# Attention into two expert layers on one core: the experts' token lists by 9 blocks of 32 places, and the first expert's second-layer weights fetched behind the first gather

## The chip, the core and the metric

The kernel runs on 1 core of a Trainium2 chip. The metric is the device time of one execution in microseconds. Five engines take part, each with its own queue of instructions: TensorE (PE in the rows; PEld is its weight load), the vector engine (DVE), ScalarE (ACT), GpSimd (POOL) and SyncE (SP), which only issues transfers here. An instruction waits for what it needs from other engines, and all that stands behind it on its engine waits with it. TensorE's granted clock is 1 at 2.4 GHz and 0.5 at 1.2 GHz.

## The reference

```
scores = q @ k.T / 8                          # 4 x 8 heads, 576 x 576, head size 64
attn = softmax over the 32 largest of each row
x = attn @ v, as 2304 tokens x 512
# first experts: 8 of them, 288 tokens each
logits = x @ w_gate                           # 2304 x 8
for idx in argsort(-logits.flatten()):        # greedy, best pairs first
    tok, e = idx // 8, idx % 8
    if tok has an expert or e has 288 tokens: continue
    assigned[tok] = e
out[tokens of e] = relu(x[tokens of e] @ w1[e]) @ w2[e]     # 512 -> 1024 -> 512
# second layer
h = out @ w_in;  result = (h * cos(h)) @ w_out              # 512 -> 2048 -> 512
```

## The kernel before

The program has four stages. Attention ends at about 453 us with x in HBM and the logits on chip. The first experts follow until about 760 us, then the second layer.

**The greedy assignment** (class `Search`) isn't done pair by pair. A round finds, by four comparisons with 24 thresholds each, how far the tokens' best logits may be taken until one expert has its 288 tokens; that expert is closed, and its number is written to `k.order` (lines 836 to 838). Each comparison is a chain: the vector engine compares (line 769), TensorE counts in 18 products (line 797), the vector engine decides (lines 801, 802), TensorE spreads the answer (line 804), and the vector engine moves the thresholds (line 808). Lines 814 to 828 then select the tokens and find the closed expert.

**The list of an expert** (`place`) follows its round. Each of the 128 partitions holds 18 tokens. The vector engine masks the expert's tokens and counts along the partition (lines 857 to 860), TensorE adds the counts of the partitions ahead (line 864), and `pos` is then the place of each token among the 288. It is split into a block and a place in it: 3 blocks of 96. Lines 873 and 874 make a mask of the block times the token's number (in two parts), line 877 a mask of the place, in two halves of 9 tokens, 18 products (line 883) put each token's number at its place, and `i96` gets it as 96 partitions x 3 columns for each expert.

**Rounds, lists and products share the engines.** `search` and `place` are generators: each `yield` is a point at which they hand over, and `tick()` runs each waiting generator up to its next one. `tick(1)` runs the first alone. Ahead of the first products only the search runs; within the products `m1` calls `tick()` four times in each of its first 8 iterations (`MID`) and twice in the later ones. So the order of instructions on each engine is fixed when the program is built.

**The products** (`m1`) run over 8 experts x 8 groups of 128 hidden features, 64 iterations. In one, `h` makes 12 products of the first layer (line 1184) and `y` 12 of the second (line 1199), two iterations later. `gather(e)` brings the expert's rows of x in three indirect transfers by GpSimd (line 1161), once the list is there; `xt` turns them with TensorE (line 1174) in one of the later iterations. ScalarE evicts what `h` made (line 1190) and the vector engine makes its low part (line 1191).

**Weights** come as float32 and are used as a high and a low part. `fetch` issues a transfer of 512 KB on SyncE's queue (line 1070) into one of three buffers (the last of expert 0's first layer goes to a buffer of its own, `r64`); `split` converts it: ScalarE makes the high part `wu` (line 1084), the vector engine or GpSimd the low part (line 1087, or 1266 where it is put off to the next iteration). Which expert's weights are fetched stands in `k.order`, which SyncE loads first (line 1058). In the order of use the first expert has four first-layer pieces, then four of the second layer, then the next expert's.

Of the kernel before, what the change touches and what calls it, by code (L numbers as in the profile page):

```python
# [34 lines left out]
E, CAP, NTOK = 8, 288, B * S  # L35
# [6 lines left out]
def constants(k, tmp):  # L42
    nc, cp = k.nc, k.cst
    G, V = nc.gpsimd, nc.vector

    def iota(name, shape, pattern, base, cm, dt=F32, pool=cp):
        t = pool.tile(shape, dt, name=name)
        G.iota(t, pattern=pattern, base=base, channel_multiplier=cm, allow_small_or_imprecise_dtypes=True)
        return t
# [15 lines left out]
    k.io3 = iota("io3", [128, 3], [[1, 3]], -100, 0)  # L65
    k.io16 = iota("io16", [128, E], [[1, E]], 16, 0)
    k.io128 = iota("io128", [128, 128], [[1, 128]], 0, 0, BF)

# [666 lines left out]
class Search:  # L735
# [36 lines left out]
    def search(s):  # L772
        k, nc, sb, rb = s.k, s.nc, s.sb, s.rb
        PEe, V, A = nc.tensor, nc.vector, nc.scalar
# [3 lines left out]
        tile = lambda nm, shape, dt=F32, nb=2: sb.tile(shape, dt, name="r" + nm, bufs=nb)  # L778
        pc, pq, pn = rb[:NS, 0:E], rb[:, E:E + 1], rb[:, 16:16 + 18 * E]
        for r in range(E):  # L780
# [8 lines left out]
            else:  # L789
# [5 lines left out]
                for z in range(NR):  # L795
# [10 lines left out]
                    if z < NR - 1:  # L806
                        w = tile("v", [128, 18])
# [21 lines left out]
            new = full  # L829
# [2 lines left out]
                V.tensor_tensor(new, full, s.full, op=OP.subtract)  # L832
            s.full = full

            t = tile("t", [128, E])
            V.scalar_tensor_tensor(t, new, 1.0, k.io16, op0=OP.mult, op1=OP.mult, accum_out=k.codes[:, r:r + 1])
            V.tensor_scalar(t[:1, 0:1], k.codes[:1, r:r + 1], -16.0, 0.0, op0=OP.add, op1=OP.max)
            V.tensor_scalar(k.order[:, r:r + 1], t[:1, 0:1], float(E - 1), None, op0=OP.min)
            s.gens.insert(0 if r == 0 else len(s.gens), s.place(r, GO if r == 0 else k.A, new))
            if r == 0:  # L840
                nc.gpsimd.tensor_copy(k.A, GO)
            s.closed += 1
# [4 lines left out]
    def place(s, r, A, new):  # L847

        k, nc, sb, rb = s.k, s.nc, s.sb, s.rb
        PEe, V = nc.tensor, nc.vector  # L850
        t18 = lambda nm, dt=F32: sb.tile([128, 18], dt, name="p" + nm)
        if r:
            yield
        while s.placed < r:
            yield
        AA = sb.tile([128, 18, E], BF, name="pAA")
        V.tensor_tensor(AA, A, new[:, None, :].to_broadcast([128, 18, E]), op=OP.mult)
        Ae, cs, pos, j, lo, jm, t1 = t18("A"), t18("cs", BF), t18("pos"), t18("j"), t18("lo", BF), t18("jm"), t18("t")
        V.tensor_reduce(Ae, AA, X, OP.add)
        V.tensor_tensor_scan(cs, k.onesf[:, :18], Ae, 0.0, OP.mult, OP.add)  # L860
        for _ in range(2 if r else 1):
            yield
        pr, pt = rb[:, 176:177], rb[:96, 180:186]
        PEe.matmul(pr, k.tri, cs[:, 17:18], start=True, stop=True)
        yield 1
        V.tensor_scalar(pos, cs, pr, -1.0, op0=OP.add, op1=OP.add)
        V.tensor_scalar(t1, pos, 96.0, None, op0=OP.is_ge)
        V.scalar_tensor_tensor(j, pos, 192.0, t1, op0=OP.is_ge, op1=OP.add)
        V.scalar_tensor_tensor(lo, j, -96.0, pos, op0=OP.mult, op1=OP.add)
        V.scalar_tensor_tensor(jm, Ae, -100.0, j, op0=OP.mult, op1=OP.add)  # L870
        yield
        ob, R = sb.tile([128, 18, 3], BF, name="pob"), sb.tile([128, 18, 2, 3], BF, name="pR")
        V.tensor_tensor(ob, jm[:, :, None].to_broadcast([128, 18, 3]), k.io3[:, None, :].to_broadcast([128, 18, 3]), op=OP.is_equal)
        V.tensor_tensor(R, ob[:, :, None, :].to_broadcast([128, 18, 2, 3]), k.tab[:, :, :, None].to_broadcast([128, 18, 2, 3]), op=OP.mult)
# [10 lines left out]
        h = sb.tile([96, 3], F32, name="ph")  # L885
        V.tensor_copy(h, pt[:, 3:])
        V.scalar_tensor_tensor(h, pt[:, :3], 64.0, h, op0=OP.mult, op1=OP.add)
        V.tensor_scalar(k.i96[:, 3 * r:3 * r + 3], h, float(NTOK - 1), None, op0=OP.min)
        s.placed += 1

        if r == 0:
            V.tensor_tensor(s.slot, pos, Ae, op=OP.mult)
        else:
            V.scalar_tensor_tensor(t1, pos, float(CAP * r), Ae, op0=OP.add, op1=OP.mult)
            V.tensor_tensor(s.slot, s.slot, t1, op=OP.add)
        if r == E - 1:
            s.gens.append(s.finish())

    def finish(s):

        k, nc, sb, rb = s.k, s.nc, s.sb, s.rb
        PEe, V = nc.tensor, nc.vector
# [14 lines left out]
        pt = rb[:, 192:228]  # L917
# [97 lines left out]
class FFN:  # L1015
# [148 lines left out]
    def m1(s, sb, ps, yT):  # L1164
# [50 lines left out]
        def fetch():  # L1215
            while s.fetched < min(last, s.done + 2 * s.RAW) and s.ready():
                e = s.units[s.fetched // 2][1]
                if rt and e < E and rt.closed <= e:
                    return
                s.fetch(1)  # L1220
# [9 lines left out]
                fetch()  # L1230

        while rt and rt.closed < 1:
            tick()
        s.half_pi, s.sin, s.least = (s.yp.tile([128, 1], F32, name=nm) for nm in ("hpi", "sin1", "least"))
        nc.gpsimd.memset(s.half_pi, math.pi / 2)
# [318 lines left out]
```

## Time and profile before

| | |
|---|---|
| median of 3 runs | 1203.29 us (1201.04 to 1208.54) |
| profiled execution | 1213.56 us, span of its rows 1211.6 us |
| TensorE busy | 1109.5 us, 92% of the span |
| vector engine busy | 1020.0 us, 84% |
| ScalarE, GpSimd busy | 768.4 us, 574.9 us |

The rows of a trace belong to the profiled execution alone. Busy time says how long an engine had an instruction in work; a matmul that waits for the array counts as busy. The share of busy time is a mean over stages with different limits. What stands in brackets behind a row is how long the engine was idle before it and whose result came last.

### The profile page before, as it was taken

How to read it: one execution, taken by the hardware profiler on the slowest of the kernel's cores; microseconds unless marked ns; L12 is line 12 of the kernel's file. 1: busy time of each engine (PE TensorE's matmuls, PEld its weight loads, DVE VectorE, ACT ScalarE, POOL GpSimd, SP SyncE). 2: the span in 40 equal slices, each digit the busy share in tenths (PEclk: the TensorE clock that was granted, in tenths of full speed). 3: DMA queues.
4: the chain of work that ended last, by engine and by line, in shares of the span. 5: the costliest groups of instructions: out<-in, count | busy, mean ns of one | idle time of the engine just before them, and what ended most of it. 6: DMA issues, size and time to landing. Idle time of an engine off the chain costs nothing.

```text
span 1211.6 us, 26491 instructions
## 1 busy us (share of the span) xinstructions
PE 1109.5 (92%) x9377; PEld 962.3 (79%) x9377; DVE 1020.0 (84%) x4139; ACT 768.4 (63%) x1505; POOL 574.9 (47%) x558
## 2 busy tenths in 40 slices
PE   6899999999999983888999899988989999999996
PEld 3677777777877763787888899977878999999995
DVE  7999999999999945877888988799999668777774
ACT  6999999999999921343444456555655555444442
POOL 5998989989889903010001110265654442212121
PEclk9999999999999985899989999999989999999998
DMA  5121121121100014345555666323322010000000
GB/s 127 34 61 37 40 67 33 33 90 46 36 18 25 2 40 142 112 155 174 181 188 175 192 202 228 127 79 105 115 86 87 1 36 10 27 27 27 27 27 29
DMA packets 61903, 98.29 MB, mean 81 GB/s; under 512 B 30912, under 2 KB 30912, under 8 KB 61248
## 3 DMA queue, kind: packets, MB, share of 16 engines
q1 hardware_dynamic: 53648, 74.47, 19.8%
q10 hardware_dynamic: 5136, 12.60, 3.2%
q0 software_dynamic: 2976, 9.44, 2.4%
q8 instruction: 75, 1.23, 0.4%
q14 instruction: 68, 0.56, 0.1%
HBM read 78.66 MB, written 17.83 MB: 80 GB/s over the span
## 4 chain that ended last, share of the span: by engine, by line
PE 44%; DVE 34%; ACT 10%; issue 6%; DMA 4%; POOL 2%; SPq 0%; DVEq 0%; POOLq 0%; ACTq 0%
PE pa L1336 11%; PE y L1384 11%; PE pa L1184 5%; PE y L1199 5%; DVE C L198 4%; DVE w L248 4%; PE sp L188 3%; DMA row<-x,i 3%; DVE wu L1266 3%; ACT sg L229 3%; PE av L317 2%; ACT P L232 2%; ACT S L192 2%; PE pt L395 2%; ACT PT L294 2%
## 5 line engine op out<-in xcount | busy, mean ns | idle before, releaser
L1336 PE MATMUL pa<-yh,wu 128*128 128x384 f32 x1152 | 222.9, 341 | 9.6 <-POOL yh L1320 5.4
L1384 PE MATMUL y<-wu,gh 128*128 128x512 f32 x864 | 221.9, 402 | 5.0 <-POOL gh L1372 4.6
L1336 PEld LDWEIGHTS pa<-yh,wu 128*128 128x128 f32 x1152 | 207.2, 190 | 20.8 <-POOL yh L1320 6.7
L236 POOL TENSOR_TENSOR W<-sg,S 128x576 f32<-128x576 bf16 x144 | 186.5, 1296 | 31.1 <-ACT sg L229 31.0
L1384 PEld LDWEIGHTS y<-wu,gh 128*128 128x128 f32 x864 | 163.9, 192 | 37.8 <-POOL gh L1372 6.2
L188 PE MATMUL sp<-kT,qz 128*128 128x288 f32 x512 | 179.4, 440 | 6.0 <-ACT S L192 4.7
L269 POOL TENSOR_SCALAR mk<-S,tall 128x576 bf16<-128x576 f32 x102 | 176.2, 1728 | 0.0
L198 DVE MAX8 C<-S 128x8 f32<-128x72 f32 x1152 | 159.5, 218 | 5.5 <-ACT S L192 5.2
L1368 ACT ACTIVATE gh<-cx 128x384 fp32r<-128x384 f32 x95 | 49.9, 525 | 143.1 <-DVE cx L1366 141.8
L1161 POOL DMA_INDIRECT row<-x,i x24 | 29.1, 1214 | 219.5 <-issue 42.4
L275 PE MATMUL pt<-ident,P 128*128 128x128 f32 x576 | 129.6, 281 | 0.0
L1184 PE MATMUL pa<-xh,wu 128*128 128x288 f32 x768 | 125.4, 315 | 0.0
L1199 PE MATMUL y<-hh,wu 128*128 128x288 f32 x768 | 121.3, 308 | 0.0
L1184 PEld LDWEIGHTS pa<-xh,wu 128*128 128x128 f32 x768 | 112.7, 202 | 3.2 <-issue 3.0
L277 PE MATMUL pt<-minus,mk 128*128 128x128 bf16 x576 | 113.9, 222 | 0.4 <-POOL mk L269 0.4
L229 ACT ACTIVATE sg<-S,tb 128x576 bf16<-128x576 f32 x144 | 111.6, 775 | 1.2
L1199 PEld LDWEIGHTS y<-hh,wu 128*128 128x128 f32 x768 | 110.5, 198 | 2.2 <-ACT hh L1190 0.8
L232 ACT ACTIVATE P<-S,nmx 128x576 f32<-128x576 f32 x144 | 110.7, 769 | 0.0
L248 DVE MAX8 w<-W 128x8 f32<-128x576 f32 x144 | 104.9, 749 | 0.1
L192 ACT ACTIVATE S<-sp 128x576 f32<-128x576 f32 x144 | 92.4, 642 | 18.2 <-PE sp L188 17.2
L1343 DVE TENSOR_SCALAR ct<-pa 128x384 f32<-128x384 f32 x95 | 52.7, 555 | 57.0 <-PE pa L1336 56.6
L275 PEld LDWEIGHTS pt<-ident,P 128*128 128x128 f32 x576 | 82.5, 143 | 21.0 <-issue 3.0
(246 smaller groups left out, 2166.9 us busy)
## 6 DMA issues: line engine op xcount, KB each, us to landing
raw<-in_moe_w_dram SPq DMA_DIRECT2D x63, 512.0 KB, 4.0
kT<-in_k_dram SPq DMA_DIRECT2D x16, 288.0 KB, 3.1
qz<-in_q_dram SPq DMA_DIRECT2D x32, 128.0 KB, 3.3
vm<-in_v_dram SPq DMA_DIRECT2D x32, 128.0 KB, 3.0
x<-xb SPq DMA_DIRECT2D x4, 1024.0 KB, 4.2
r<-in_moe_w_in_dram ACTq DMA_DIRECT2D x8, 512.0 KB, 5.0
r<-in_moe_w_out_dram ACTq DMA_DIRECT2D x8, 512.0 KB, 4.8
half<-in_moe_w_in_dram SPq DMA_DIRECT2D x8, 512.0 KB, 3.8
```

The costliest lines, as they stand in the source:

```text
L188: s.nc.tensor.matmul(s.SP[j][:, c, :288], lh, s.KT[p][:, o + c * 288:o + c * 288 + 288], start=True, stop=True)
L198: s.nc.vector.max(c[:, e, :], s.SS[j][:, 72 * e:72 * e + 72])
L229: A.activation(s.SG[j], s.SS[j], AF.Sign, bias=s.TB[g][:, u:u + 1], scale=-EPS1, accum_out=s.SUM[g][:, u:u + 1])
L232: A.activation(s.PB[j // 2][:, S * (j % 2):S * (j % 2) + S], s.SS[j], AF.Exp, bias=s.NMX[g][:, u:u + 1])
L236: s.nc.gpsimd.tensor_tensor(s.W[j], s.SG.pop(j), s.SS[j], op=OP.mult)
L248: V.max(w8[:, u, :], s.W.pop(4 * g + u))
L269: (nc.vector if kind == "d" else nc.gpsimd).tensor_scalar(m, s.SS[j], T, None, op0=OP.is_lt)
L275: PEe.matmul(out, s.PB[d][:, o:o + 128], s.k.ident, is_transpose=True, start=True, stop=m is None)
L1184: PEe.matmul(p, w[:, a, f * 128:(f + 1) * 128], XH[e, c][:, b, :], start=n == 0, stop=n == 11)
L1199: PEe.matmul(Y[e][m], w[:, a, o + m * 128:o + (m + 1) * 128], t[:, b, :], start=f == 0 and i == 0, stop=f == 7 and i == 2)
L1336: s.nc.tensor.matmul(p, w[:, a, f * 128:(f + 1) * 128], s.YH[q, c][:, b, :], start=n == 0, stop=n == 11)
L1384: PEe.matmul(O[q][m], g[:, a, m * 128:(m + 1) * 128], w[:, b, c:c + 512], start=first and j == 0, stop=last and j == 2)
```

## The change

The list of an expert is split into 9 blocks of 32 places. Block and place are a shift and a bit mask of the integer `pos`. The mask of the block and its product with the token numbers have 9 columns for 3, the mask of the place has 32 for 96 and is made in one instruction, so the generator has one `yield` less. The 18 products give 32 places x 9 blocks, and three instructions write them to `i96` so that it holds what it held before.

For the first closed expert the three instructions that write its number (`which`) come behind the count along the partition, ahead of which they stood.

Behind the first gather SyncE gets a copy of one number from the third gathered block to a tile `mark` that nothing reads. The fetches of the second-layer weights of the first expert, which were issued one by one in the loop over the first four conversions, now come after the loop. The loop converts the low parts of the first three pieces on the vector engine, and the fourth on GpSimd; before it was the second and third on the vector engine. It calls `tick()` six times, before four.

```diff
-            t = tile("t", [128, E])
-            V.scalar_tensor_tensor(t, new, 1.0, k.io16, op0=OP.mult, op1=OP.mult, accum_out=k.codes[:, r:r + 1])
-            V.tensor_scalar(t[:1, 0:1], k.codes[:1, r:r + 1], -16.0, 0.0, op0=OP.add, op1=OP.max)
-            V.tensor_scalar(k.order[:, r:r + 1], t[:1, 0:1], float(E - 1), None, op0=OP.min)
+            def which(r=r, new=new):
+                t = tile("t", [128, E])
+                V.scalar_tensor_tensor(t, new, 1.0, k.io16, op0=OP.mult, op1=OP.mult, accum_out=k.codes[:, r:r + 1])
+                V.tensor_scalar(t[:1, 0:1], k.codes[:1, r:r + 1], -16.0, 0.0, op0=OP.add, op1=OP.max)
+                V.tensor_scalar(k.order[:, r:r + 1], t[:1, 0:1], float(E - 1), None, op0=OP.min)
+                s.closed += 1
+
+            if r:
+                which()
+            else:
+                s.which = which
...
         V.tensor_tensor_scan(cs, k.onesf[:, :18], Ae, 0.0, OP.mult, OP.add)
+        if r == 0:
+            s.which()
...
-        V.tensor_scalar(t1, pos, 96.0, None, op0=OP.is_ge)
-        V.scalar_tensor_tensor(j, pos, 192.0, t1, op0=OP.is_ge, op1=OP.add)
-        V.scalar_tensor_tensor(lo, j, -96.0, pos, op0=OP.mult, op1=OP.add)
+        V.tensor_scalar(j, pos, 5, None, op0=OP.logical_shift_right)
+        V.tensor_scalar(lo, pos, 31, None, op0=OP.bitwise_and)
...
-        oh = [s.big(2 + h, 9 * 96, BF).rearrange("p (a b) -> p a b", a=9) for h in range(2)]
-        for h in range(2):
-            V.tensor_tensor(oh[h], k.io128[:, None, :96].to_broadcast([128, 9, 96]),
-                            lo[:, 9 * h:9 * h + 9, None].to_broadcast([128, 9, 96]), op=OP.is_equal)
-            yield
+        oh = s.big(2, 18 * 32, BF).rearrange("p (a b) -> p a b", a=18)
+        V.tensor_tensor(oh, k.io128[:, None, :32].to_broadcast([128, 18, 32]), lo[:, :, None].to_broadcast([128, 18, 32]), op=OP.is_equal)
+        yield
...
-            PEe.matmul(pt, oh[q // 9][:, q % 9, :], R[:, q].rearrange("p a b -> p (a b)"), start=q == 0, stop=q == 17)
+            PEe.matmul(pt, oh[:, q, :], R[:, q].rearrange("p a b -> p (a b)"), start=q == 0, stop=q == 17)
...
-        V.tensor_scalar(k.i96[:, 3 * r:3 * r + 3], h, float(NTOK - 1), None, op0=OP.min)
+        for u in range(3):
+            V.tensor_scalar(k.i96[32 * u:32 * u + 32, 3 * r:3 * r + 3], h[:, u::3], float(NTOK - 1), None, op0=OP.min)
...
             s.gather(0)
+
+            nc.sync.dma_start(s.mark, s.XG[0][2][:1, :1])
             for n in range(4):
-                s.split(1, eng=V if n in (1, 2) else None)
-                fetch()
+                s.split(1, eng=V if n < 3 else None)
                 tick()
+                if n in (1, 2):
+                    tick()
+            fetch()
```

How this moves instructions is seen at three places. The vector engine at the end of the first round and the start of the first list, before (`rt,codes` and `order` are the expert's number, `pAA`, `pA` and `pcs` the mask and the counts, `ppos` the place):

```order
L828 TENSOR_SCALAR rfull<-rem 128x8
L836 SCALAR_TENSOR_TENSOR rt,codes<-rfull,io_94 128x8
L837 TENSOR_SCALAR rt<-codes 1x1
L838 TENSOR_SCALAR order<-rt 1x1
L857 TENSOR_TENSOR pAA<-rGO,rfull 128x144
L859 TENSOR_REDUCE pA<-pAA 128x18
L860 SCALAR_TENSOR_TENSOR pcs<-onesf,pA 128x18
L866 TENSOR_SCALAR ppos<-pcs,pa_8690 128x18
```

The same place now:

```order
L828 TENSOR_SCALAR rfull<-rem 128x8
L863 TENSOR_TENSOR pAA<-rGO,rfull 128x144
L865 TENSOR_REDUCE pA<-pAA 128x18
L866 SCALAR_TENSOR_TENSOR pcs<-onesf,pA 128x18
L837 SCALAR_TENSOR_TENSOR rt,codes<-rfull,io_94 128x8
L838 TENSOR_SCALAR rt<-codes 1x1
L839 TENSOR_SCALAR order<-rt 1x1
L874 TENSOR_SCALAR ppos<-pcs,pa_8690 128x18
```

The three instructions of the number now stand between the counts and the place, where TensorE adds up the counts in between.

SyncE's queue at the first gather, before (`r_8839` is the last first-layer piece of the first expert, the pieces of 128x2x512 are of its second layer):

```order
L1070 DMA raw<-in_moe_w_dram 128x1024
L1070 ISA
L1070 DMA r_8839<-in_moe_w_dram 128x1024
L1070 ISA
L1070 DMA raw<-in_moe_w_dram 128x2x512
```

The same place now:

```order
L1078 DMA raw<-in_moe_w_dram 128x1024
L1078 ISA
L1078 DMA r_8851<-in_moe_w_dram 128x1024
L1256 DMA mark<-row 1x1
L1078 ISA
L1078 DMA raw<-in_moe_w_dram 128x2x512
```

The copy to `mark`, which needs the third gathered block, stands ahead of the first second-layer piece and all later fetches.

The vector engine at the list of the second closed expert, expert 1 in the order of use, before (`yh_9272` is the second half of the mask of the place, of which the first stands three rows ahead, `wu` low parts of weights, `yh_8693`, `rv`, `rov` and `rfe` the next round's search, `hh` the low part of first-layer results, `i_65` the list):

```order
L1266 TENSOR_TENSOR wu_9277<-raw,wu_9277 128x1024
L1266 TENSOR_TENSOR wu_9279<-raw,wu_9279 128x1024
L877 TENSOR_TENSOR yh_9272<-io_96,plo 128x864
L801 SCALAR_TENSOR_TENSOR rov<-pa_8690,rem 24x8
L802 TENSOR_SCALAR rfe<-rov 24x1
L1191 SCALAR_TENSOR_TENSOR hh<-pa_9287,hh 128x288
L808 TENSOR_SCALAR rv<-rv,pa_8690 128x18
L769 TENSOR_TENSOR yh_8693<-rv,steps 128x432
L886 COPY ph<-pa_8690 96x3
L887 SCALAR_TENSOR_TENSOR ph<-pa_8690,ph 96x3
L888 TENSOR_SCALAR i_65<-ph 96x3
```

The same place now:

```order
L885 TENSOR_TENSOR yh_9254<-io_96,plo 128x576
L808 TENSOR_SCALAR rv<-rv,pa_8690 128x18
L769 TENSOR_TENSOR yh_8693<-rv,steps 128x432
L1199 SCALAR_TENSOR_TENSOR hh<-pa_9210,hh 128x288
L801 SCALAR_TENSOR_TENSOR rov<-pa_8690,rem 24x8
L802 TENSOR_SCALAR rfe<-rov 24x1
L893 COPY ph<-pa_8690 32x9
L894 SCALAR_TENSOR_TENSOR ph<-pa_8690,ph 32x9
L896 TENSOR_SCALAR i_65<-ph 32x3 x3
L902 SCALAR_TENSOR_TENSOR pt<-ppos,pA 128x18
L903 TENSOR_TENSOR slot<-slot,pt 128x18
L1279 TENSOR_TENSOR wu_9328<-raw,wu_9328 128x1024
```

The two conversions stood between the halves of the mask and now stand behind the finished list.

## Rows read from the trace of the kernel before

**Rows 1.** Busy times by stage; the columns stand in the first line.
```profile
core 0: us, PE busy (x) PEld busy (x) DVE busy (x) ACT busy (x) POOL busy (x), PEclk, DMA share, GB/s
...
453.00:481.00 28.00, 8.35 (x127) 6.77 (x127) 16.79 (x62) 5.26 (x7) 9.04 (x8) 0.51 0.42 129
481.00:760.00 279.00, 251.38 (x2133) 238.15 (x2132) 229.47 (x585) 132.20 (x234) 27.24 (x24) 0.93 0.56 180
```

**Rows 2.** Timeline between attention and experts: start, us, engine, line, operation, [idle before].
```profile
464.33 0.17 DVE L836 SCALAR_TENSOR_TENSOR rt<-rfull,io 128x8 f32<-128x8 bf16 x1
...
467.14 0.27 DVE L874 TENSOR_TENSOR pR<-pob,tab 128x108 bf16<-128x108 bf16 x1
...
467.33 2.02 DVE L877 TENSOR_TENSOR yh<-io,plo 128x864 bf16<-128x864 bf16 x2
...
468.43 1.85 PE L883 MATMUL pa<-pR,yh 128*96 128x6 bf16 x18 [2.65 <-DVE yh L877]
...
470.70 0.17 DVE L888 TENSOR_SCALAR i<-ph 96x3 int32<-96x3 f32 x1
...
471.78 1.12 POOL L1161 DMA_INDIRECT row<-x,i  x1 [8.05 <-issue]
...
473.35 14.24 SPq L1070 DMA_DIRECT2D raw<-in_moe_w_dram  x4
...
474.43 1.95 POOL L1161 DMA_INDIRECT row<-x,i  x1 [0.31 <-issue]
...
474.45 0.61 PE L797 MATMUL pa<-rO,yh 128*24 128x8 bf16 x18 [4.17 <-DVE yh L769]
...
476.41 2.35 POOL L1087 TENSOR_TENSOR wu<-raw,wu 128x1024 fp32r<-128x1024 f32 x1
...
478.92 2.31 PE L1174 MATMUL y<-ident,row 96*128 96x96 f32 x11 [3.37 <-DMA row<-x,i]
...
480.94 1.79 PE L1184 MATMUL pa<-xh,wu 128*128 128x288 f32 x6
```

**Rows 3.** Tile row: landing of the first gather's first and third transfer.
```profile
DMA to landing us min/median/max: 3.3/3.3/3.3
...
DMA to landing us min/median/max: 4.9/4.9/4.9
```

**Rows 4.** The page's DMA issues: count, size, median us to landing.
```profile
raw<-in_moe_w_dram SPq DMA_DIRECT2D x63, 512.0 KB, 4.0
```

**Rows 5.** Waits of TensorE in the experts' stage: us in total, times, longest.
```profile
PE pa L1174 <- DMA row<-x,i: 10.1, 8, 3.0
...
PE pa L804 <- DVE rfe L802: 6.9, 6, 2.7
```

**Rows 6.** Timeline ahead of expert 1's list, the columns as in rows 2.
```profile
501.19 1.85 PE L1184 MATMUL pa<-xh,wu 128*128 128x288 f32 x12
...
501.97 1.06 ACT L1084 ACTIVATE wu<-raw 128x1024 fp32r<-128x1024 f32 x1 [3.29 <-DMA raw<-in_moe_w_dram]
...
505.69 1.23 DVE L1266 TENSOR_TENSOR wu<-raw,wu 128x1024 fp32r<-128x1024 f32 x1 [0.71 <-ACT wu L1084]
...
506.83 1.05 DVE L877 TENSOR_TENSOR yh<-io,plo 128x864 bf16<-128x864 bf16 x1
...
508.18 0.16 PE L804 MATMUL pa<-rfe,ones 24*128 24x1 bf16 x1 [2.70 <-DVE rfe L802]
```

**Rows 7.** Timeline at the lists of experts 2 and 6, columns as before.
```profile
539.44 0.97 PE L883 MATMUL pa<-pR,yh 128*96 128x6 bf16 x18
...
552.36 0.79 PE L1174 MATMUL pa<-ident,row 96*128 96x96 f32 x4 [3.02 <-DMA row<-x,i]
...
552.86 3.21 PE L1184 MATMUL pa<-xh,wu 128*128 128x288 f32 x12
...
699.38 0.42 PE L1174 MATMUL pa<-ident,row 96*128 96x96 f32 x1 [1.87 <-DMA row<-x,i]
```

More of the change, by code (lines that the diff above doesn't have):

```diff
@@ L64, in constants @@
     k.steps = iota("steps", [128, NS], [[-1, NS]], -1, 0, BF)
-    k.io3 = iota("io3", [128, 3], [[1, 3]], -100, 0)
+    k.io9 = iota("io9", [128, 9], [[1, 9]], -100, 0)
     k.io16 = iota("io16", [128, E], [[1, E]], 16, 0)
@@ L841, in search @@
                 nc.gpsimd.tensor_copy(k.A, GO)
-            s.closed += 1
             yield
@@ L857, in place @@
         V.tensor_tensor(AA, A, new[:, None, :].to_broadcast([128, 18, E]), op=OP.mult)
-        Ae, cs, pos, j, lo, jm, t1 = t18("A"), t18("cs", BF), t18("pos"), t18("j"), t18("lo", BF), t18("jm"), t18("t")
+        Ae, cs, pos, j, lo, jm, t1 = t18("A"), t18("cs", BF), t18("pos", I32), t18("j", I32), t18("lo", I32), t18("jm"), t18("t")
         V.tensor_reduce(Ae, AA, X, OP.add)
         V.tensor_tensor_scan(cs, k.onesf[:, :18], Ae, 0.0, OP.mult, OP.add)
+        if r == 0:
+            s.which()
         for _ in range(2 if r else 1):
             yield
-        pr, pt = rb[:, 176:177], rb[:96, 180:186]
+        pr, pt = rb[:, 176:177], rb[:32, 180:198]
         PEe.matmul(pr, k.tri, cs[:, 17:18], start=True, stop=True)
@@ L866, in place @@
         V.tensor_scalar(pos, cs, pr, -1.0, op0=OP.add, op1=OP.add)
-        V.tensor_scalar(t1, pos, 96.0, None, op0=OP.is_ge)
-        V.scalar_tensor_tensor(j, pos, 192.0, t1, op0=OP.is_ge, op1=OP.add)
-        V.scalar_tensor_tensor(lo, j, -96.0, pos, op0=OP.mult, op1=OP.add)
+        V.tensor_scalar(j, pos, 5, None, op0=OP.logical_shift_right)
+        V.tensor_scalar(lo, pos, 31, None, op0=OP.bitwise_and)
         V.scalar_tensor_tensor(jm, Ae, -100.0, j, op0=OP.mult, op1=OP.add)
         yield
-        ob, R = sb.tile([128, 18, 3], BF, name="pob"), sb.tile([128, 18, 2, 3], BF, name="pR")
-        V.tensor_tensor(ob, jm[:, :, None].to_broadcast([128, 18, 3]), k.io3[:, None, :].to_broadcast([128, 18, 3]), op=OP.is_equal)
-        V.tensor_tensor(R, ob[:, :, None, :].to_broadcast([128, 18, 2, 3]), k.tab[:, :, :, None].to_broadcast([128, 18, 2, 3]), op=OP.mult)
-        oh = [s.big(2 + h, 9 * 96, BF).rearrange("p (a b) -> p a b", a=9) for h in range(2)]
-        for h in range(2):
-            V.tensor_tensor(oh[h], k.io128[:, None, :96].to_broadcast([128, 9, 96]),
-                            lo[:, 9 * h:9 * h + 9, None].to_broadcast([128, 9, 96]), op=OP.is_equal)
-            yield
+        w = s.big(3, 3 * 18 * 9, BF)
+        ob, R = w[:, :162].rearrange("p (a b) -> p a b", a=18), w[:, 162:].rearrange("p (a z b) -> p a z b", a=18, z=2)
+        V.tensor_tensor(ob, jm[:, :, None].to_broadcast([128, 18, 9]), k.io9[:, None, :].to_broadcast([128, 18, 9]), op=OP.is_equal)
+        V.tensor_tensor(R, ob[:, :, None, :].to_broadcast([128, 18, 2, 9]), k.tab[:, :, :, None].to_broadcast([128, 18, 2, 9]), op=OP.mult)
+        oh = s.big(2, 18 * 32, BF).rearrange("p (a b) -> p a b", a=18)
+        V.tensor_tensor(oh, k.io128[:, None, :32].to_broadcast([128, 18, 32]), lo[:, :, None].to_broadcast([128, 18, 32]), op=OP.is_equal)
+        yield
         if r:
@@ L882, in place @@
         for q in range(18):
-            PEe.matmul(pt, oh[q // 9][:, q % 9, :], R[:, q].rearrange("p a b -> p (a b)"), start=q == 0, stop=q == 17)
+            PEe.matmul(pt, oh[:, q, :], R[:, q].rearrange("p a b -> p (a b)"), start=q == 0, stop=q == 17)
         yield 1
-        h = sb.tile([96, 3], F32, name="ph")
-        V.tensor_copy(h, pt[:, 3:])
-        V.scalar_tensor_tensor(h, pt[:, :3], 64.0, h, op0=OP.mult, op1=OP.add)
-        V.tensor_scalar(k.i96[:, 3 * r:3 * r + 3], h, float(NTOK - 1), None, op0=OP.min)
+        h = sb.tile([32, 9], F32, name="ph")
+        V.tensor_copy(h, pt[:, 9:])
+        V.scalar_tensor_tensor(h, pt[:, :9], 64.0, h, op0=OP.mult, op1=OP.add)
+        for u in range(3):
+            V.tensor_scalar(k.i96[32 * u:32 * u + 32, 3 * r:3 * r + 3], h[:, u::3], float(NTOK - 1), None, op0=OP.min)
         s.placed += 1
@@ L916, in finish @@
             yield
-        pt = rb[:, 192:228]
+        pt = rb[:, 200:236]
         for h in range(2):
@@ L1232, in m1 @@
         while rt and rt.closed < 1:
-            tick()
+            tick(1)
         s.half_pi, s.sin, s.least = (s.yp.tile([128, 1], F32, name=nm) for nm in ("hpi", "sin1", "least"))
+        s.mark = s.yp.tile([1, 1], F32, name="mark")
         nc.gpsimd.memset(s.half_pi, math.pi / 2)
```

## The prediction

> **What bounds the kernel now.** I read the busy times by stage first. The change touches the 28 us between attention and the experts, where TensorE works 8.35 us at a granted clock of 0.51, that is mostly at 1.2 GHz, and the 279 us of the experts' products, where TensorE is busy 251 us, the vector engine 229 us, and the clock is 0.93 [rows 1]. The first is a plain chain; the second has slack, since neither engine is full.
>
> The chain, read from the timeline: the vector engine ends the first search round, writes the expert's number from 464.33, builds the list of its tokens (mask and table products until 467.33, then two comparisons of 864 elements, 2.02 us together), TensorE adds 18 products, 1.85 us, and the indices stand from 470.70 [rows 2]. GpSimd starts the three gathers at 471.78, the last at 474.43, and TensorE, which had begun to turn the rows, goes on from 478.92 and has its first expert product at 480.94 [rows 2]. The third gather needs 4.9 us from issue to landing and the first 3.3 [rows 3]: the last landing, 474.43 + 4.9 = 479.3, is what the start waits for.
>
> In the experts' stage I read the waits of TensorE. They name two things: rows that a gather has not landed yet, 10.1 us in eight waits, and the search's answers from the vector engine, of which the largest line has 6.9 us in six [rows 5]. Then I looked at what stands before the two longest. At 508.18 TensorE waits 2.70 us for the search; the vector engine was held there by weight conversions whose transfers came late (ScalarE had waited 3.29 us for one), and by a second comparison of 1.05 us for the list queued behind them [rows 6]. At 552.36 it waits 3.02 us for rows; the 12 products behind it take 3.21 us, against 1.85 for 12 at 501.19 [rows 6, 7], so a wait is often paid a second time through the clock.
>
> **The change part by part.** Where I add times up for the first list, they start at 464.33.
>
> *Expert number behind the scan.* Three small instructions, the first of 0.17 us [rows 2], so 0.5 us together, go behind the scan, where the vector engine waits for one column of TensorE's anyway. I take 0.3 us off the chain (ends 0 and 0.5). In exchange the expert's weights are asked for about 0.7 us later: that is covered as long as their conversions are done when the rows land, and I return to it.
>
> *The list by 9 blocks of 32.* One arithmetic instruction less: -0.2. The table product of 108 elements takes 0.27 and a comparison of 864 half of 2.02 [rows 2], so some 0.98 ns for each further element: mask of 162 elements 0.32, table product of 324 elements 0.48, against about 0.5 now for the pair: +0.3. One comparison of 576 elements, 0.73, for two of 1.01: -1.3. The 18 products now have 32 columns; the nearest rows are 0.61 us for 18 of 24 columns and 1.85 for 18 of 96, by columns 0.75 [rows 2], but the nine first of the old ones lay beside the second comparison, so only -0.15. The index write becomes three writes of 32 partitions, of 0.17 us each [rows 2]: +0.35. Sum -1.0; with the number moved -1.3, and I keep 1.1 (ends 0.4, if the products stay near 1.85, and 1.6).
>
> TensorE's side of it counts again for each later expert: 0.97 us when the clock is up [rows 7] against some 0.6, and on the vector engine two comparisons of 1.05 become one of 0.73 with the other parts unchanged in sign, a net 0.8 less. Seven experts: 2.6 us on one engine, 5.6 on the other. One engine is the bound at a time, so I take 3 us (ends 0 and 5.6).
>
> *Fetch behind the gather.* The SyncE queue gets a four-byte copy out of the third gathered block, and so waits until it has landed; behind it stand the fetches of the first expert's second-layer weights, and nothing else wants that queue then. It gives the gather the transfer engines: only one of those fetches, at 473.35, was issued inside the gather in the trace [rows 2], so one transfer is removed, not four. The third landing should go from 4.9 toward the first one's 3.3 [rows 3]: I take 0.8 of the 1.6 (ends 0 and 1.6). The price: these weights are asked for at about 477 and not 473.35. A fetch of this size lands 4.0 us after its issue in the median [rows 4], so at 481, 483 if it is slow, and its conversion stands behind the eviction of the first 12 products, which begin at 479 and end at 482 at the low clock (3.21 us [rows 7]). That cover is just enough: I cost the hold at nothing, and at 1 to 2 us if the fetch is slow, since ScalarE's later evictions queue behind the conversion.
>
> *Conversions.* The first low part goes from GpSimd (2.35 us, at 476.41 because the gathers stand ahead of it) to the vector engine [rows 2]. It is done before the rows land, so the start does not wait for it. The third gather shows GpSimd's issue stretched to 1.95 us where the first took 1.12 [rows 2]; more vector work inside the gather could do that to another one: I set 0, with 1 us in the range. The Trainium skill ("SBUF — State Buffer", section "SBUF: two separate sides") speaks against this move: GpSimd writes the gather's descriptors through a port pair that it shares with the vector engine, and one fully blocks the other. By that rule each conversion that falls on an issue would hold it for up to its own length, and the start's gain would be 1 us instead of 2. The 1.95 us would fit that; no row here shows what held it.
>
> So the first expert product comes at 480.94 - 1.1 - 0.8 = 479.0: **1.9 us**, ends -0.6 and 3.2.
>
> *Order of search and products.* This is where most of it lies. Two more search steps are put into the gather's wait, and each later list takes one step fewer. Read off the new order: the 18 products of expert 1's list stand after 5 groups of first-layer products, not 6, and ahead of the pair of weight conversions, which before stood between the list's two comparisons. So the late transfers [rows 6] no longer hold up the list or its gather. The 2.70 us go; the pair is then late for the next search step, so some of it returns. From the products of the list to the first use of the rows there were two to three groups of each layer for experts 3 to 5 and three for expert 6, and it is now three, three to four, four, and four to five. A group of 12 is up to 1.85 us [rows 6], so one group of each layer more is some 3.5 us more for the rows to land in. For those experts the waits for rows should end; for expert 6 the last of three waits alone is 1.87 [rows 7]. For experts 1 and 2 the distance hardly grows, so their waits stay. Out of 10.1 us [rows 5] I take 6 away, and 1.5 of slow clock behind them; out of the search's waits 4. Together with the 3 us above this is 14.5, but an engine that no longer waits for rows meets the search's next answer sooner, and the vector engine is already busy 229 of 279 us [rows 1]. I keep half: **7 us** (ends 0 and 14.5).
>
> **The rivals.** *The waits only move* (0.25). The vector engine is 82% busy, and each search round is a chain of round trips between it and TensorE. For it: the 6.9 us in six waits spread over all experts [rows 5]. Against: the rows' waits are not the vector engine's. Then only the start stays, with about 1 us of shorter lists: 3 us, or 1200.
>
> *All of it counts* (0.17): rows' waits and the clock behind them go and nothing comes back: 1.9 + 14.5, some 16 us, or 1187. Against: two experts keep their distance.
>
> *Conversions stand in the search's way* (0.06), the side on which it is slower. In the new order the pair for the second-layer weights stands right between the search's selection and its sum for expert 1; were that so for all seven, and TensorE there first, each would cost a pair of conversions, 2 x 1.23 us [rows 6], and 1.4 of slow clock as at 552.86 (3.21 against 1.85) [rows 6, 7]: 27 us, less the 9 gained, makes 1221. It decides from the point at which the conversions' weights land later than the selection. Against: for the later experts the order has one conversion there, as before.
>
> *The fetch does not do what it says* is inside these: with one transfer of 512 KB out of the way, the start gains 1.1 and not 1.9, and the time moves by less than 1.
>
> **How the numbers follow.** The profiled execution took 1213.56 us, of which the span is 1211.6. 1.9 + 7 = 8.9 off it gives 1204.7. The median of the runs, 1203.29 (1201.04 to 1208.54), lies 10.3 below the profiled execution, and some of the profiled waits may not be in each run; I take the difference over and round: 1203.3 - 9 = **1194**, chance 0.52. About 1% (12 us) is what a measurement of this kernel can tell from no change. The likeliest case has its own range of 1188 to 1200, and a third of its chance lies below 1191.3, with all of the second rival: 0.35 for faster. Slower by over 1% is the third rival: 0.06. Within 1%: 0.59. The range of 1183 to 1204 leaves out the third rival and some of the second's far end.
>
> **What would show it.** Right: first expert product about 9.4 us after the start of the last index write, now 10.2, and about 14.7 us after the expert's number is begun, not 16.6; GpSimd's first gather near 470.7; the 18 products near 0.6 us; no wait of over 2 us just ahead of expert 1's list; waits for rows of some 4 us in total, none at expert 6. Wrong: a gather issue of 2 us beside the conversions with the last landing still at 479; waits of TensorE for the search well above the present 6.9 us in their largest line, which would say that the vector engine took back what the rows gave; or ScalarE waiting for the second-layer weights at the first expert's second group, the price of the hold.

## The result and the profile after

The changed kernel took 1191.59 us (median of 4 runs, 1190.06 to 1194.68); the kernel before took 1205.91 beside it (4 runs, 1201.04 to 1216.20). The ratio is 0.9857, with a 95% interval of 0.9819 to 0.9894: faster by 1.4%. The profiled execution of the changed kernel took 1191.52 us, its span 1189.7.

Where the time came from is read by cutting both traces at the same three events: the first product of the first layer, the first product of the second layer, and the end. Between the first two lie the 64 iterations of the experts' products. The kernel before, busy times by stage (the columns are those of [rows 1]):

```profile
core 0: us, PE busy (x) PEld busy (x) DVE busy (x) ACT busy (x) POOL busy (x), PEclk, DMA share, GB/s
400.00:449.00 49.00, 45.00 (x650) 35.93 (x650) 34.35 (x184) 28.82 (x63) 23.44 (x21) 0.90 0.01 2
480.94:768.19 287.25, 259.63 (x2195) 246.40 (x2193) 234.49 (x591) 136.94 (x242) 28.81 (x26) 0.93 0.57 181
```

The same view of the changed kernel; the first and the last row answer to [rows 1]:

```profile
453.00:481.00 28.00, 10.37 (x139) 8.59 (x139) 18.26 (x59) 5.87 (x8) 6.47 (x7) 0.50 0.48 152
475.60:743.34 267.74, 248.22 (x2194) 235.67 (x2193) 229.15 (x592) 135.91 (x242) 26.97 (x26) 0.96 0.59 196
481.00:760.00 279.00, 260.47 (x2258) 248.01 (x2258) 237.67 (x603) 142.29 (x253) 29.62 (x27) 0.97 0.57 187
```

The experts' stage went from 287.25 to 267.74 us for the same number of matmuls (2195 and 2194): 19.5 us less. TensorE is busy 11.4 us less in it and idle 8.1 us less, and its granted clock rose from 0.93 to 0.96. From the start of the search to the first product there are 27.7 us before and 26.4 after, and from the first second-layer product to the end of the span 443.4 and 446.4. The spans differ by more than that, by 21.9 us, because the kernel before began its search 4 us later in this profile, after a stretch at a clock of 0.90 in which it runs the same code as the changed one. A second profile of the kernel before (`before_again`, below) began it at the changed kernel's time, so those 4 us are not the change's.

The waits of TensorE in the stage (us in total, times, longest), answering to [rows 5]:

```profile
PE pa L797 <- DVE yh L769: 7.4, 5, 2.5
PE pa L804 <- DVE ppos L874: 2.4, 2, 1.4
PE pa L820 <- DVE rGO L816: 2.1, 2, 1.2
...
PE pa L1182 <- DVE xh L1184: 1.2, 1, 1.2
...
PE pa L1192 <- DVE xh L1184: 1.0, 1, 1.0
PE pa L804 <- DVE rfe L802: 0.5, 1, 0.5
PE pa L1182 <- DMA row<-x,i: 0.4, 1, 0.4
```

The waits for rows fell from 10.1 us to 0.4. The waits for the vector engine, all lines together, were 17.0 and are 18.4 us. Of these, 2.2 are for the low part of the turned rows (`xh`); those for the search and its lists are 16.2, a little less than before. Among them the line that led before (`rfe`, 6.9) is down to 0.5, and the comparison `yh` leads with 7.4.

The start, read from the timeline of the changed kernel. It answers to [rows 2]; line 1169 is the gather, 1182 the turning of the rows, 1192 the first-layer products, 1256 the copy to `mark`:

```profile
460.27 0.23 DVE L863 TENSOR_TENSOR pAA<-rGO,rfull 128x144 bf16<-128x144 bf16 x1
...
462.88 0.75 DVE L885 TENSOR_TENSOR yh<-io,plo 128x576 bf16<-128x576 bf16 x1
...
463.68 0.65 PE L890 MATMUL pa<-yh,yh 128*32 128x18 bf16 x18 [2.39 <-DVE yh L885]
...
464.82 0.50 DVE L896 TENSOR_SCALAR i<-ph 32x3 int32<-32x3 f32 x3
...
466.23 1.12 POOL L1169 DMA_INDIRECT row<-x,i  x1 [6.55 <-issue]
...
467.25 1.22 DVE L1095 TENSOR_TENSOR wu<-raw,wu 128x1024 fp32r<-128x1024 f32 x1 [1.73 <-ACT wu L1092]
467.65 1.62 POOL L1169 DMA_INDIRECT row<-x,i  x1 [0.30 <-DMA raw<-in_moe_w_dram]
...
469.58 0.92 POOL L1169 DMA_INDIRECT row<-x,i  x1 [0.30 <-issue]
...
473.71 2.18 PE L1182 MATMUL y<-ident,row 96*128 96x96 f32 x12
473.72 2.36 POOL L1095 TENSOR_TENSOR wu<-r,wu 128x1024 fp32r<-128x1024 f32 x1 [3.22 <-ACT wu L1092]
473.82 2.30 DVE L808 TENSOR_SCALAR rv<-rv,pa 128x18 f32<-128x18 f32 x1 [0.25 <-PE pa L804]
473.91 0.75 SPq L1256 DMA_DIRECT2D mark<-row  x1
...
475.60 0.59 PE L1192 MATMUL pa<-xh,wu 128*128 128x288 f32 x1
...
477.18 1.57 PE L1192 MATMUL pa<-xh,wu 128*128 128x288 f32 x5 [1.00 <-DVE xh L1184]
...
481.42 1.05 ACT L1092 ACTIVATE wu<-raw 128x1024 fp32r<-128x1024 f32 x1
```

From the first instruction of the list's chain to the end of the last index write there are 5.05 us (465.32 − 460.27), before 6.54 (470.87 − 464.33). From there to the first gather 0.91 us, as before. From the first gather's start to the third's 3.35 us, before 2.65; from the third's start to the landing 4.3 (`mark` is issued as soon as the block is there), before 4.9.

The place ahead of expert 1's list, answering to [rows 6]:

```profile
489.71 2.35 DVE L1279 TENSOR_TENSOR wu<-raw,wu 128x1024 fp32r<-128x1024 f32 x2
...
495.70 0.60 PE L797 MATMUL pa<-rO,yh 128*24 128x8 bf16 x18 [2.51 <-DVE yh L769]
...
501.21 0.60 PE L890 MATMUL pa<-yh,yh 128*32 128x18 bf16 x18
...
502.49 0.50 DVE L896 TENSOR_SCALAR i<-ph 32x3 int32<-32x3 f32 x3
...
503.34 2.36 DVE L1279 TENSOR_TENSOR wu<-raw,wu 128x1024 fp32r<-128x1024 f32 x2
...
503.74 1.62 POOL L1169 DMA_INDIRECT row<-x,i  x1 [27.66 <-PE pa L804]
...
506.57 0.60 PE L797 MATMUL pa<-rO,yh 128*24 128x8 bf16 x18 [1.85 <-DVE yh L769]
```

The 18 products no longer wait, the pair of conversions stands behind the finished list, and the next search step pays for the pair with 1.85 us. The gather comes 2.5 us after the products (503.74 − 501.21). An earlier pair (489.71) now stands ahead of the end of the search round, and TensorE waits 2.51 us for the next round's first comparison (495.70), where it waited 0.36 before.

### The profile page after: what moved, and what is told of

The parts are those of the page before. It is cut to its first block, busy times and chain, and to the rows that moved or that the text cites. A ratio compares the mean times of both kernels' runs of the same rounds, so it can differ in the third digit from the quotient of the medians.

```text
span 1189.7 us, 26492 instructions
## 1 busy us (share of the span) xinstructions
PE 1097.0 (92%) x9377; PEld 949.3 (80%) x9377; DVE 1015.9 (85%) x4140; ACT 766.9 (64%) x1505; POOL 569.0 (48%) x557
## 4 chain that ended last, share of the span: by engine, by line
PE 45%; DVE 37%; ACT 8%; issue 6%; DMA 2%; POOL 1%; SPq 0%; DVEq 0%; POOLq 0%; ACTq 0%
PE pa L1349 11%; PE y L1397 10%; PE pa L1192 6%; PE y L1207 5%; DVE w L248 5%; DVE C L198 4%; PE sp L188 4%; DVE wu L1279 3%; PE av L317 3%; ACT sg L229 2%; ACT P L232 2%; DVE ct L1357 2%; ACT S L192 2%; PE pt L395 2%; DVE row L1128 2%
## 5 line engine op out<-in xcount | busy, mean ns | idle before, releaser
L1349 PEld LDWEIGHTS pa<-yh,wu 128*128 128x128 f32 x1152 | 207.9, 190 | 19.5 <-POOL yh L1333 4.9
L1169 POOL DMA_INDIRECT row<-x,i x24 | 26.6, 1108 | 200.4 <-DVE slot L903 83.1
L1207 PE MATMUL y<-hh,wu 128*128 128x288 f32 x768 | 117.5, 302 | 0.0
L1192 PEld LDWEIGHTS pa<-xh,wu 128*128 128x128 f32 x768 | 110.3, 197 | 5.2 <-issue 2.3
L1207 PEld LDWEIGHTS y<-hh,wu 128*128 128x128 f32 x768 | 107.0, 192 | 2.0 <-ACT hh L1198 1.2
```

Of the source, the lines that this page charges most:

```text
L1192: PEe.matmul(p, w[:, a, f * 128:(f + 1) * 128], XH[e, c][:, b, :], start=n == 0, stop=n == 11)
L1207: PEe.matmul(Y[e][m], w[:, a, o + m * 128:o + (m + 1) * 128], t[:, b, :], start=f == 0 and i == 0, stop=f == 7 and i == 2)
L1349: s.nc.tensor.matmul(p, w[:, a, f * 128:(f + 1) * 128], s.YH[q, c][:, b, :], start=n == 0, stop=n == 11)
```

## The experiments

The theory was that the gain is one of order: the rows of each later expert are asked for earlier, so TensorE stops waiting for them. Two rivals: the cheaper list gives it (fewer vector and TensorE microseconds for each expert), or the start does (the gather alone on the transfer engines, conversions off GpSimd). The change has parts that carry one of these each. Each edit is shown against the kernel that it starts from. Ratios are to the kernel before on the same chip, with the 95% interval. "Stage" is the experts' stage of one profile, cut as above; "waits for the search" are here all of TensorE's waits for the vector engine in it.

**The two further search steps alone.** The kernel before, with only this:

```diff
                 s.split(1, eng=V if n in (1, 2) else None)
                 fetch()
                 tick()
+                if n in (1, 2):
+                    tick()
```

> Before with only the two more ticks in the gather's wait (six for four). Order theory (each list stands earlier against the products, so rows land in time): TensorE's waits for gathered rows fall from 10.1 us to 5 or less, ratio about 0.993 (5 to 9 us). Work theory (the gain is the cheaper list): nothing is cheaper, ratio 0.999 to 1.002. Start theory (the gain is the first product's earlier start): ratio 1.000.

0.9907 (0.9879 to 0.9936), 1197.88 us. Stage 273.4 us, waits for rows 4.3, for the search 16.6. The start took 27.6 us, as before. Two calls that do no work of their own give two thirds of the whole gain: they shift where each list stands among the products.

**The list alone**, with its one `yield` less, on the old start (old loop, number ahead of the count, no `mark`). Against the changed kernel, with the loop and the number put back:

```diff
-            if r:
-                which()
-            else:
-                s.which = which
+            which()
...
-            nc.sync.dma_start(s.mark, s.XG[0][2][:1, :1])
             for n in range(4):
-                s.split(1, eng=V if n < 3 else None)
+                s.split(1, eng=V if n in (1, 2) else None)
+                fetch()
                 tick()
-                if n in (1, 2):
-                    tick()
-            fetch()
```

> Before with only the list by 9 blocks of 32 and its one yield less; expert number, fetches, conversions and ticks as before. Order theory: the lists stand half as much earlier as with all of the change, ratio 0.990 to 0.994, waits for rows 5 us or less. Work theory: nearly all of the change's gain, ratio 0.986 to 0.988. Start theory: the shorter first chain alone, 1 to 1.5 us, ratio 0.999.

0.9871 (0.9841 to 0.9902), 1195.87 us. Stage 265.0 us at a clock of 0.98, waits for rows 6.2, for the search 12.2; but its start took 29.4. Nearly all of the gain is here without any of the start's edits. By what was expected, this ratio speaks for the cheaper list and the waits for rows speak for the order; the next two runs part them.

**The list's work and its `yield` apart.** `work_alone` is the kernel above with a second `yield` behind the comparison, so that the order has as many steps as before. `yield_alone` is the kernel before with one `yield` behind both comparisons in place of one behind each:

```diff
             V.tensor_tensor(oh[h], k.io128[:, None, :96].to_broadcast([128, 9, 96]),
                             lo[:, 9 * h:9 * h + 9, None].to_broadcast([128, 9, 96]), op=OP.is_equal)
-            yield
+        yield
```

> The list by 9 blocks of 32 alone, with the yield that it saves put back: all products and lists stand as before (expert 1's list after 6 groups, expert 3's after 19), but each list costs the vector engine about 0.8 us and TensorE 0.35 us less. Order theory: waits for rows stay at 8 to 12 us, ratio 0.996 to 0.999. Work theory: as the list alone, 0.986 to 0.990.

> Before with only one yield less: both comparisons of 96 places in one step, nothing cheaper; the lists stand where the list by 9 blocks alone puts them. Order theory: waits for rows 6 us or less, ratio 0.988 to 0.993. Work theory: 2 us of comparisons in one step hold up the search, ratio 0.999 or more.

`work_alone` 0.9963 (0.9934 to 0.9992), 1206.62 us; `yield_alone` 0.9916 (0.9887 to 0.9945), 1199.48. The two ratios multiply to 0.9879, the list alone has 0.9871: within the intervals they add up. So order is about two thirds of the list's gain and the cheaper work one third; each interval is 0.6% wide, so the shares are rough. Their profiles show that they work on different waits. For `yield_alone`, the waits of TensorE in the stretch 470 to 790:

```profile
PE pa L797 <- DVE yh L769: 19.1, 9, 10.5
PE pa L1174 <- DMA row<-x,i: 3.5, 4, 1.2
```

And its busy times in the stage:

```profile
481.92:752.31 270.39, 250.95 (x2195) 238.07 (x2194) 233.66 (x591) 136.53 (x242) 28.33 (x25) 0.97 0.57 191
```

The same two views of `work_alone`:

```profile
PE pa L797 <- DVE yh L769: 15.1, 6, 11.7
PE pa L1178 <- DMA row<-x,i: 12.8, 12, 2.8
```

```profile
481.50:758.80 277.30, 253.98 (x2195) 239.59 (x2194) 228.82 (x591) 136.84 (x242) 29.42 (x25) 0.95 0.56 185
```

(The longest waits, 10.5 and 11.7, lie ahead of the stage, in the first gather.) The stage is 16.9 us shorter with one `yield` less and 10.0 with the cheaper list; both kernels lose some 2 us of it in a start of 30.0 and 29.6 us, for which the last section has a reason. One `yield` less takes the waits for rows from 10.1 to 3.5 and leaves the search's in the stage at 15.3. The cheaper list leaves the rows' at 12.8 and takes the search's from 17.0 to 9.9. How long the rows have shows in the time from the third gather's start to the first turning of a row (where TensorE waits for that row, the wait is part of the time), for experts 1 to 6: before 4.7, 2.3, 5.9, 4.9, 4.7, 4.7 us; `work_alone` 3.7, 2.0, 3.7, 2.9, 3.1, 3.4; `yield_alone` 5.5, 4.8, 2.6, 6.6, 6.1, 6.7; the changed kernel 8.2, 4.0, 6.2, 7.1, 10.3, 10.7. A second profile of the kernel before has 4.1, 3.8, 5.9, 3.3, 5.1, 4.1, so 1.5 us for one expert tell nothing. Expert 6 in the kernel before:

```profile
691.36 0.92 POOL L1161 DMA_INDIRECT row<-x,i  x1 [0.30 <-issue]
...
696.05 0.30 PE L1174 MATMUL pa<-ident,row 96*128 96x96 f32 x1 [1.67 <-DMA row<-x,i]
```

And in the changed kernel:

```profile
665.98 1.03 POOL L1169 DMA_INDIRECT row<-x,i  x1 [0.30 <-issue]
...
676.69 0.41 PE L1182 MATMUL pa<-ident,row 96*128 96x96 f32 x3
```

**The copy behind the gather**, alone on the kernel before (with the fetches behind the loop, conversions as they were), and taken out of the changed kernel:

```diff
+            nc.sync.dma_start(s.mark, s.XG[0][2][:1, :1])
             for n in range(4):
                 s.split(1, eng=V if n in (1, 2) else None)
-                fetch()
                 tick()
+            fetch()
```

```diff
-            nc.sync.dma_start(s.mark, s.XG[0][2][:1, :1])
             for n in range(4):
                 s.split(1, eng=V if n < 3 else None)
+                fetch()
                 tick()
```

> Before with only the copy behind the third gathered block, and the second-layer fetches behind it; conversions, ticks, lists as before. Order and work theory: the third landing comes 0.5 to 1.6 us earlier, ratio 0.999 to 1.000. Start theory: ratio 0.995 or less. If the hold costs, ScalarE waits for the second-layer weights and the ratio is 1.001 to 1.003.

> After without the hold: no copy, the fetches in the loop as before. Order and work theory: 0.986 to 0.988, within 1 us of after. Start theory: it loses most of the gain, ratio 0.993 or more.

Alone 1.0002 (0.9978 to 1.0026), 1211.68 us; the changed kernel without it 0.9844 (0.9818 to 0.9871), 1193.01, against 0.9857 and 0.9859 with it. The whole shows no effect either way. The single traces point to an earlier third landing, most clearly in one of them. Without it, TensorE's rows at the start:

```profile
476.24 0.42 PE L1182 MATMUL y<-ident,row 96*128 96x96 f32 x1
477.53 0.42 PE L1182 MATMUL y<-ident,row 96*128 96x96 f32 x1 [0.87 <-DMA row<-x,i]
480.48 1.86 PE L1182 MATMUL y<-ident,row 96*128 96x96 f32 x10 [2.52 <-DMA row<-x,i]
```

The third gather had started at 472.14, so its block took 8.3 us to land with three weight fetches issued from 471.07 on; with the copy 4.3 us (changed kernel) and 3.1 (`hold_alone`, 473.44 to 476.53). The first product came after 30.4 us without the copy. But with the old loop the block took only 3.6 to 4.9 us in six profiles without the copy, and with the changed kernel's loop 4.1 to 5.6 in the six profiles that have it, so the larger part rests on this one trace. These 4 us of one trace are not found in the medians, whose intervals leave room for some 3 us either way; how often the landing is that late stays open.

**The start's other edits.** The fourth low part on the vector engine too; the changed kernel without the two further steps; and both:

```diff
-                s.split(1, eng=V if n < 3 else None)
+                s.split(1, eng=V)
                 tick()
```

```diff
                 tick()
-                if n in (1, 2):
-                    tick()
```

> After with the fourth low part on the vector engine too, so GpSimd converts nothing beside the gather's end. If GpSimd's conversion held up the vector engine's small operation (2.30 us for 0.24), that operation falls to 0.3 us, the wait of 1.0 us inside the first product goes, and the first product's 12 end about 1 us earlier: ratio 0.984 to 0.986, at most 0.001 from after. If that operation waited for something else, it stays at 2 us and the added 1.23 us on the vector engine make the start later.

> After without the two more ticks: the list by 9 blocks, its one yield less, the hold, the number moved and the first low part on the vector engine. The lists stand as in the list alone, half as much earlier as in after. Order theory, if more is better: ratio 0.988 to 0.990, worse than after. If the one yield already lets most rows land (the list alone had its experts' stage at 265.0 us, after 267.7), the ticks add nothing: ratio 0.984 to 0.987.

> As the run without the two more ticks, with the fourth low part on the vector engine too, so that nothing of GpSimd's holds up the search's small operation at the start: the first product about 26 to 27 us after the search's start, experts' stage 264 to 267 us, ratio 0.983 to 0.986, the best of all if the ticks add nothing.

0.9850 (0.9817 to 0.9882), 0.9844 (0.9815 to 0.9873) and 0.9862 (0.9831 to 0.9893): none differs from the changed kernel. Without the steps the stage has 6.3 us of waits for rows and 12.8 for the search, with them 0.4 and 18.4 (16.2 without `xh`), and it takes 267.1 and 267.7 us. So the steps, worth 0.9% on the old list, are worth nothing on the new one: they and the missing `yield` both move the list forward, and what the second of them takes from the rows the search gives back.

**The changed kernel and the kernel before again.** No edit; the run called `no_hold_again` is the changed kernel itself, a third time.

> After, unchanged, on the same chip as the others: ratio 0.983 to 0.989 by its first measurement.

> After once more, unchanged, for its clock at the end of attention, ahead of all that the change touches: 1.00 in 400 to 449 us as twice before, the search's start at 449, if the program sets it; other values if chance does.

> Before once more, unchanged, for the same: granted clock 0.90 in 400 to 449 us and the search's start at 453 if the program sets it; 0.97 or 1.00 and 449 to 452 if chance does, and then some 1 to 4 us of the profiles' difference do not belong to the change.

The changed kernel again 0.9859 (0.9827 to 0.9891), 1192.49 us, and 1192.65 in a single run; the kernel before 1211.37 in a single run. Stages of the changed kernel 268.4 and 267.3 us, of the kernel before 287.0: what the first pair of profiles showed holds. The start of the changed kernel took 26.6 and 27.8 us, of the kernel before 27.9. And the kernel before had run at full clock ahead of the search this time:

```profile
400.00:449.00 49.00, 44.10 (x677) 35.51 (x675) 36.68 (x196) 30.11 (x65) 24.10 (x21) 1.00 0.06 22
```

## Why the prediction was right, and what it mis-sized

The forecast was 1194 us, within a range of 1183 to 1204; the time was 1191.59. The direction and the place were right: most came from the order in the experts' stage. The size was not, and its likeliest outcome, a change within 1% (0.59), did not come; the 0.35 for faster did. The forecast took 9 us off, and the change took 14 off in the first comparison and 17 to 19 in the later ones. That the time came out near is in part luck: the three runs of the kernel before that the forecast started from, 1203.29, lie low, and later medians are 1210 to 1212. By its ratio, 0.986, the result is that of the rival in which all counts (1187 of 1203.29 is 0.9865).

*The step that failed* is the halving: "I keep half: 7 us" of 14.5, because TensorE would meet the search's next answer sooner. The stage gave 19.5 in the profiles. By its own terms:
- Rows' waits, 6 us of 10.1: measured 9.7.
- The slow clock behind them, 1.5 us: measured about 8.8, and this is the largest error. TensorE's busy time fell by 11.4 us. The products of the seven lists went from 8.22 to 4.21 us, of which 2.6 is their price at the higher clock (seven times 0.97 − 0.60); the other 1.4, with 5.3 in the experts' products of both layers (125.41 + 117.64 to 123.91 + 113.86) and 2.1 in the turning of the rows (14.24 to 12.12), adds up to 8.8 us that matmuls took less for the same work. The granted clock agrees, as an estimate: a mean of 0.93 between levels of 1 and 0.5 is 14% of 287 us, or 40 us, at 1.2 GHz, and 0.96 is 8% of 268, or 21 us; half of the difference is 9 us. The forecast priced the clock at one group of 12 products that it had seen at 3.21 us in place of 1.85.
- The search's waits, 4 us: measured 0.8 (17.0 to 16.2; in the second profiles 18.3 before, 16.4 and 16.3 after). Here the reasoning behind the halving was right in kind: the line `rfe` fell from 6.9 to 0.5 and the line `yh` rose from 5.1 to 7.4. Another 2.2 came in new, the waits for the low part of the turned rows (2.0 and 1.2 in the second and third profile).
- The lists, 3 us: 2.6 in products alone, and by `work_alone` 0.4% of the whole, 4.5 us, what its longer start costs taken off.

9.7 + 8.8 + 0.8 − 2.2 + 2.6 = 19.7, against the 19.5 between the cuts. This splits up what was measured and is no test of it; that the 8.8 is the clock rests on the estimate from the granted clock.

*"For experts 1 and 2 the distance hardly grows, so their waits stay."* Wrong for expert 1: its rows had 4.7 us and have 8.2, and no wait is left. For expert 2 the distance was rightly read: 2.3 and 3.8 us in two profiles before, 3.8 to 4.0 in three after; yet its waits fell, from 4.0 and 1.4 us to 0.4 to 0.7. The forecast counted groups of products from the list's 18 products on. The gather starts when the vector engine has written the indices, and for expert 1 that came 3.75 us behind the products before (512.02 − 508.27) and comes 2.5 now.

*The start, 1.9 us.* The list's chain gave 1.5 (forecast 1.1, ends 0.4 and 1.6): the 18 products took 0.65 us, the comparison 0.75, the three index writes 0.50. The third landing gave 0.6 (forecast 0.8), but the third gather started 0.7 us later after the first than before, which the forecast had put at nothing. So from the last index write to the first product (the third of the three begins at about 465.15) there are 10.45 us where 9.4 were forecast and 10.24 stood. In all 1.3 us in this pair of profiles: 15.3 us from the chain's first instruction (460.27) on, 16.6 before, 14.7 forecast. The Trainium skill ("SBUF — State Buffer", section "SBUF: two separate sides") has an exclusive lock on the port pair of GpSimd and the vector engine. By that rule the forecast's start was 1 us; the trace agrees: the second gather's issue took 1.62 us beside the conversion of 467.25 to 468.47, the other two 1.12 and 0.92. (The third began 0.31 us ahead of the conversion at 469.89; they took 0.92 and 1.22 us, neither more than elsewhere.) Over three profiles of the changed kernel the start takes 26.4 to 27.8 us, over two of the kernel before 27.7 and 27.9, so its gain of some 1 us is hardly more than its own scatter.

*The cover of the hold.* As forecast, it cost nothing: ScalarE converts the first second-layer weights at 481.42 without waiting.

*The third rival*, the conversions between the search's selection and its sum, came true once, in part, for expert 1, though the pair's weights were not late: the vector engine makes the selection at 489.21, the pair from 489.71 to 492.06 and the sum at 492.13, has no gap until the comparison ends at 495.64, and TensorE waits 2.51 us for that. The list's own pair, behind it, cost the 1.85 us ahead of 506.57. The price for all seven experts, 27 us, did not come: apart from these two the search's longest wait in the stage is 1.74.

Not settled: the second layer and what follows took 443.4 and 445.2 us before, 446.2 to 446.4 in the changed kernel, so some 1 to 3 us may be given back there; no run was made for it. It need not be the change's: `hold_alone`, which leaves lists and order as they were, has 446.0.

## What to carry to other kernels

When the order of a program is fixed by hand-overs, remove or add one hand-over before making the work cheaper: here one `yield` less, with no arithmetic changed, was worth 0.8%, and two calls that do nothing of their own 0.9%, while the work itself was worth 0.4%. Measure a gather's time to land from its issue, which is the end of the index chain, to the first use, and not in groups of products. And where a stage's mean clock is below 1, price a removed wait by the clock of the whole stage, not by the one slow group behind it: here the clock gave about as much as the waits.

## What the runs showed of the hardware

A small vector instruction can be held by a GpSimd conversion to that one's end. The move of the thresholds (`rv`, 128x18, 0.24 us at other times) took 2.30 us in the changed kernel and ended at 476.12, where GpSimd's conversion ended at 476.08 (473.72 + 2.36). In the second profile of the changed kernel it took 2.14 us, and in the third, where it was done before GpSimd's conversion began (475.44 and 476.16), 0.24. Two further kernels show it, with two conversions in a row. `ticks_alone`:

```profile
472.69 5.02 DVE L808 TENSOR_SCALAR rv<-rv,pa 128x18 f32<-128x18 f32 x1 [0.25 <-PE pa L804]
473.01 2.35 POOL L1087 TENSOR_TENSOR wu<-raw,wu 128x1024 fp32r<-128x1024 f32 x1
...
475.31 2.36 POOL L1087 TENSOR_TENSOR wu<-r,wu 128x1024 fp32r<-128x1024 f32 x1
```

`list_alone`, where it is the first setting of the thresholds (line 791, 0.29 us at other times):

```profile
472.86 5.37 DVE L791 TENSOR_SCALAR rv<-rm,span 128x18 f32<-128x18 f32 x1
473.54 2.35 POOL L1090 TENSOR_TENSOR wu<-raw,wu 128x1024 fp32r<-128x1024 f32 x1
475.85 2.33 POOL L1090 TENSOR_TENSOR wu<-r,wu 128x1024 fp32r<-128x1024 f32 x1
```

They end at 477.71 and 478.23, GpSimd's second conversions at 477.67 and 478.18: each time 0.04 or 0.05 us later. `work_alone` and `yield_alone` have the 5.37 us too, and with `list_alone` their starts took 29.4 to 30.0 us: in `list_alone` the third block had landed at 475.66 (472.04 + 3.62), and TensorE began to turn rows at 479.47, behind the search's products that had waited for these thresholds. With the fourth conversion on the vector engine (`fourth_on_dve`) the same instruction takes 0.24 us again, and the first products follow one another without the 1.00 us gap that stands ahead of 477.18 in the changed kernel:

```profile
474.13 0.24 DVE L808 TENSOR_SCALAR rv<-rv,pa 128x18 f32<-128x18 f32 x1 [0.25 <-PE pa L804]
474.93 1.22 DVE L1095 TENSOR_TENSOR wu<-r,wu 128x1024 fp32r<-128x1024 f32 x1
475.98 2.16 PE L1192 MATMUL pa<-xh,wu 128*128 128x288 f32 x6
```

In the first product's time this was worth nothing (475.98 against 475.60); the first 12 products ended 0.6 us sooner (480.42 against 481.03), and in the whole it was worth nothing that the runs can tell.
